# Exclusive sums of the fourth unit by one logarithm, and engine orders written out as tables, in a gated recurrence with a squared-ReLU layer behind it

## The chip, the cores and the metric

The kernel runs on one core of one Trainium2 chip. The metric is the device time of one execution in microseconds (us), lower is better. The engines are PE (matrix products), DVE (vector), ACT (activation functions, also copies), POOL (general purpose) and SP, which here only issues DMA transfers. POOL issues some transfers as well. Each engine runs its own list of instructions strictly in order and waits on semaphores for the others.

## The reference

A recurrence with a decay for each channel runs over 768 tokens, for 4 batches, 8 heads and a head size of 48. Its output, as 3072 tokens of 384 values, goes through two dense layers with a squared ReLU between them.

```python
for t in range(S):
    state = alpha[:, :, t, :, None] * state + np.einsum('bhd,bhe->bhde', k[:, :, t], v[:, :, t])
    y[:, :, t] = np.einsum('bhd,bhde->bhe', q[:, :, t], state)
...
h = x @ w_in            # 384 -> 2048
g = np.maximum(h, 0.0) ** 2
return (g @ w_out).astype(np.float32)      # 2048 -> 384
```

Inputs and output are float32; inside, products are taken in bf16.

## The kernel before

**Tiling.** The work is cut into 12 *units* of 256 tokens: unit g is batch g % 4, time chunk g // 4. A partition holds two neighbouring tokens, j = 0 and 1, for all heads. Units 0 to 3 are the first chunk of each batch, so the "fourth unit" is unit 3. Every step of a unit is an operation with a short name; the number behind it is the unit, and further numbers are parts of it.

**Front of a unit** (`front`, `decays_by_pair`, lines 670 to 765). `lda ldk ldq ldv` load alpha, k, q, v into one of four `raw` buffers (L568; on SP, for unit 2 on POOL). The decay from the start of a chunk to each token is the exponential of a running sum of log alpha. From unit 2 on: `pr` multiplies alpha of both tokens of a pair (L675 on DVE, L677 on POOL); `ln` takes the logarithm (L678); `m1i` multiplies by a triangular matrix of ones on PE (L684), which gives the inclusive sums in a PSUM bank `psW`; `ei`, `ea` and `ec` are exponentials of them (L695, L697, L700); `bk` multiplies by alpha of j = 1 (L704). The queries of j = 0 need the *exclusive* sums, and there are two ways to them, chosen by `if g < RATIO` at L706 with `RATIO = 4` (L424):

- units 2 and 3: a second triangular product `m1s` with the strict triangle (L684 again, `lstr`), `es` as its exponential (L709), and `aq`, a multiplication by alpha of j = 0 (L713);
- units 4 to 11: `lm`, the logarithm of alpha of j = 1 (L717), `lb`, the inclusive sums less that (L719, on DVE), and `es` as the exponential (L721).

Unit 0 is done by halves of the heads (`front_by_heads`, L584 to L641), unit 1 by token (L646 to L667). `vc` casts v to bf16 (L613, L741 on POOL, L742 on ACT). `ekm` and `eqm` multiply keys and queries by their exponentials (L620, L746, L751, on DVE). `tr` transposes them: on PE with an eviction `et` for units 0 to 2 (L632 with L639 and L641, L774 with L781 and L783), by DMA on SP for the others (L762).

**Attention and state.** `p` are the scores (L940), `mk` masks them (L951, on DVE), `kv` are the products for the state (L811), `sa`, `sc` and `sd` bring the state up to date (L904 to L917). `y` is the output of the recurrence (L832 and L843, in units 0 to 2 L872 and L879). From y2 on, one y holds the kv of the next unit too, so y2 waits for vc3. `xe` evicts the output (L971), `xt` transposes it (L986 on PE, L992 by DMA), `xv` evicts that for units 0 to 3 (L998, L1000).

**Dense layers.** For each unit eight parts `s1` (L1042, six matmuls each) go into two PSUM banks in turn, `re` is the ReLU (L1050 on ACT, L1052 on DVE), `sq` squares two parts at once, or one for the last two (1024 or 512 elements, L1060 on DVE, L1063 on POOL, L1064 on ACT). `s2` is the second layer (L1089, four matmuls each, first index the half of the tokens), `oe` evicts (L1097, L1099), `out` stores. The second half of the tokens of the last unit is cut in two (L1012 to L1021). The weights come by POOL in two parts each (`win`, `wout`, L539); the first four `s1` of a unit read only the first part of `win`.

**What sets the order.** `add` records operations with their reads and writes, engines that could run them (`alts`) and a priority. `schedule` (L159) runs a list scheduler over estimated costs, by priority plus a shift for each name from a table `SHIFT` (L49), and so picks engine and order. `fill` (L271) puts matmuls of zeros into early gaps of PE (L1143). `place` (L298) derives the semaphore waits; the order is fixed when the program is built. Loads also have gates of their own (`AFTER`, L1119, and `BEHIND`, L551): `win` waits until alpha of unit 1 has landed, POOL's loads of unit 2 until v of unit 1 has, the loads of unit 3 until the first `wout` has, and from unit 5 on a load waits for a step of the unit before (alpha for its `ln`, k for its `ekm`, q and v for its `tr0`).

Of the kernel before, what the change touches and what calls it, by code (L numbers as in the profile page):

```python
# [2 lines left out]

# [3 lines left out]
ALU = mybir.AluOpType  # L7
# [7 lines left out]
class Op:  # L15


    __slots__ = ("alts", "eng", "fn", "cost", "prio", "deps", "idx", "lag", "sem", "start", "end", "pos", "name",
                 "users", "ndeps", "mode", "ready", "land")

    def __init__(self, alts, prio, name):
        self.alts, self.prio, self.name = alts, prio, name
        self.eng = self.fn = self.cost = None
        self.deps = {}
        self.lag = 0
        self.sem = None
        self.users = []
        self.pos = None
        self.mode = ("F", "F")
        self.ready = 0.0  # L30
        self.start = self.end = self.land = None


class Program:

    HOP = 35
    PE_LATENCY = 170
    DMA_FIRST = {"sp": 1300, "act": 1300, "pool": 2000}  # L40
    PACKET = (("win", 172), ("wout", 490), ("ld", 22), ("tr", 18), ("xt", 18), ("out", 125))
    SBUF_ONLY = ("pr", "bk", "aq", "ekm", "eqm", "sq", "sb", "sd")
    BIAS = {"pool": 300}
    DMA_LAST = {"sp": 800, "act": 800, "pool": 1900}
    SWITCH = 95
    HALVED = {"qks": 3, "kqt": 3, "raw": 3, "ek": 3, "eq": 3, "acm": 2, "laf": 2}
    AFFINITY = 2500

    SHIFT = {  # L49
# [55 lines left out]
    }  # L105

# [1068 lines left out]
```

## Time and profile before

| | |
|---|---|
| median of 3 runs | 175.18 us (174.51 to 175.5) |
| span of the profiled execution | 174.47 us (the page rounds to 174.5) |
| around the span, median less span | 0.71 us |
| granted TensorE clock | 1.000 |
| first matmul of the dense layers (L1042) | starts at 18.46 us |
| last matmuls (L1012), by the chain of waits | 169.49 to 172.14 us |

The profiled execution's own time isn't given apart from its span; the median stands for it. A row of the page's groups reads: line, engine, operation, output<-inputs, shape, count, busy us, mean ns of one, idle time before them and who ended it. In the timeline, a row is: start us, length us, engine, line, operation, in brackets how long the engine was idle before and who released it. The chain of waits is the chain of work that ended last, followed back from the end; its rows are: start us, us, what. PE overlaps matmuls, so what one costs is read from start to start and not from its length.

### The profile page before, as it was taken

How to read it: one execution, taken by the hardware profiler on the slowest of the kernel's cores; microseconds unless marked ns; L12 is line 12 of the kernel's file. 1: busy time of each engine (PE TensorE's matmuls, PEld its weight loads, DVE VectorE, ACT ScalarE, POOL GpSimd, SP SyncE). 2: the span in 40 equal slices, each digit the busy share in tenths (PEclk: the TensorE clock that was granted, in tenths of full speed). 3: DMA queues.
4: the chain of work that ended last, by engine and by line, in shares of the span. 5: the costliest groups of instructions: out<-in, count | busy, mean ns of one | idle time of the engine just before them, and what ended most of it. 6: DMA issues, size and time to landing. Idle time of an engine off the chain costs nothing.

```text
span 174.5 us, 5094 instructions
## 1 busy us (share of the span) xinstructions
PE 169.1 (97%) x2237; PEld 130.5 (75%) x2237; DVE 121.3 (70%) x197; ACT 117.6 (67%) x211; POOL 18.8 (11%) x28
## 2 busy tenths in 40 slices
PE   7989999999999999999999999999999999999994
PEld 2556898856886697777788886778788697688773
DVE  5497799797967869866778966868849726322230
ACT  3848698868869569768768757378668564566440
POOL 3159010022102120000100000000200000000000
DMA  5999999979998999798998897999899690040022
GB/s 139 324 297 190 274 303 216 230 208 280 274 229 125 274 235 188 200 222 151 278 212 211 228 196 180 275 201 251 201 214 208 115 196 4 0 135 4 10 80 90
DMA packets 74743, 33.36 MB, mean 191 GB/s; under 512 B 71649, under 2 KB 71905, under 8 KB 74721
## 3 DMA queue, kind: packets, MB, share of 16 engines
q1 hardware_dynamic: 73184, 28.32, 71.4%
q0 software_dynamic: 1536, 4.72, 12.1%
q8 instruction: 17, 0.28, 0.7%
q14 instruction: 6, 0.04, 0.1%
HBM read 25.17 MB, written 4.72 MB: 171 GB/s over the span
## 4 chain that ended last, share of the span: by engine, by line
PE 56%; DMA 26%; ACT 6%; DVE 4%; SPq 3%; POOL 2%; issue 1%
PE psO L1089 22%; PE psWH L1042 22%; DMA raw<-in_v_dram 9%; DMA wout<-in_moe_w_out_dram 8%; DMA raw<-in_alpha_dram 5%; DMA raw<-in_q_dram 5%; SPq L568 3%; PE psO L1143 2%; POOL raw L568 2%; ACT rr L1050 2%; PE psX L843 2%; PE psX L1012 2%; ACT vbf L742 1%; PE psZ L811 1%; PE psX L832 1%; PE psX L940 1%
## 5 line engine op out<-in xcount | busy, mean ns | idle before, releaser
L1042 PE MATMUL psWH<-xt,win 128*128 128x256 bf16 x576 | 73.9, 275 | 0.5 <-ACT rr L1050 0.2
L1042 PEld LDWEIGHTS psWH<-xt,win 128*128 128x128 bf16 x576 | 65.0, 145 | 6.2 <-DVE rr L1052 1.6
L1089 PE MATMUL psO<-wout,gt 128*128 128x384 bf16 x368 | 68.9, 326 | 0.0
L1050 ACT ACTIVATE rr<-psWH 128x512 bf16<-128x512 f32 x83 | 48.9, 596 | 21.5 <-PE psWH L1042 20.0
L1089 PEld LDWEIGHTS psO<-wout,gt 128*128 128x128 bf16 x368 | 34.8, 98 | 18.3 <-DVE gt L1060 0.2
L1060 DVE TENSOR_TENSOR gt<-rr 128x1024 bf16<-128x1024 bf16 (+1 forms) x47 | 28.4, 608 | 25.1 <-ACT rr L1050 24.5
L951 DVE TENSOR_TENSOR pm<-psX,caus 128x1024 bf16<-128x1024 f32 x12 | 14.6, 1220 | 2.4 <-PE psZ L940 2.1
L951 DVE TENSOR_TENSOR pm<-psZ,caus 128x1024 bf16<-128x1024 f32 x12 | 14.6, 1216 | 1.5 <-PE psZ L940 1.4
L1097 ACT ACTIVATE osb<-psO 128x384 f32<-128x384 f32 x19 | 9.3, 489 | 6.8 <-PE psO L1089 6.3
L971 ACT ACTIVATE xbf<-psX 128x768 bf16<-128x768 f32 x12 | 9.7, 806 | 5.0 <-PE psX L832 4.1
L746 DVE TENSOR_TENSOR qks<-raw,eq 128x384 bf16<-128x384 f32 x18 | 10.3, 605 | 3.0 <-DMA raw<-in_q_dram 3.0
L1143 PE MATMUL psO<-zero 128*128 128x512 bf16 (+1 forms) x37 | 10.5, 417 | 1.3 <-DVE zero L489 1.3
L741 POOL CAST vbf<-raw 128x768 bf16<-128x768 f32 x4 | 3.7, 930 | 71.5 <-DMA raw<-in_v_dram 71.5
L1064 ACT ACTIVATE gt<-rr 128x512 bf16<-128x512 bf16 (+1 forms) x13 | 10.8, 828 | 0.4
L751 DVE TENSOR_TENSOR qks<-raw,ek 128x768 bf16<-128x768 f32 x11 | 10.7, 969 | 0.4 <-ACT ek L663 0.3
L1052 DVE TENSOR_SCALAR rr<-psWH 128x512 bf16<-128x512 f32 x13 | 8.9, 687 | 2.0 <-PE psWH L1042 1.6
L742 ACT ACTIVATE vbf<-raw 128x768 bf16<-128x768 f32 x7 | 5.9, 845 | 3.5 <-DMA raw<-in_v_dram 3.5
L717 ACT ACTIVATE la<-raw 128x384 f32<-128x384 f32 x8 | 4.2, 523 | 5.3 <-DMA raw<-in_alpha_dram 5.2
L1143 PEld LDWEIGHTS psO<-zero 128*128 128x128 bf16 x37 | 3.5, 108 | 4.6 <-issue 1.9
L906 DVE TENSOR_TENSOR smd<-psZ,sbd 128x384 bf16<-128x384 f32 x8 | 4.4, 554 | 3.4 <-PE psX L832 3.4
L675 DVE TENSOR_TENSOR prd<-raw 128x384 f32<-128x384 f32 x7 | 4.0, 569 | 2.9 <-DMA raw<-in_alpha_dram 2.9
L678 ACT ACTIVATE lab<-prd 128x384 bf16<-128x384 f32 x10 | 5.2, 520 | 1.1 <-POOL prd L677 0.6
(115 smaller groups left out, 165.9 us busy)
## 6 DMA issues: line engine op xcount, KB each, us to landing
raw<-in_alpha_dram SPq DMA_DIRECT2D x11, 384.0 KB, 4.2
raw<-in_k_dram SPq DMA_DIRECT2D x11, 384.0 KB, 5.1
raw<-in_q_dram SPq DMA_DIRECT2D x11, 384.0 KB, 4.2
raw<-in_v_dram SPq DMA_DIRECT2D x11, 384.0 KB, 4.8
out_dram<-osb SPq DMA_DIRECT2D x11, 384.0 KB, 4.3
win<-in_moe_w_in_dram POOLq DMA_DIRECT2D x2, 768.0 KB, 9.9
wout<-in_moe_w_out_dram POOLq DMA_DIRECT2D x2, 768.0 KB, 15.2
raw<-in_alpha_dram POOLq DMA_DIRECT2D x1, 384.0 KB, 9.7
```

The costliest lines, as they stand in the source:

```text
L746: add("dve", lambda e, j=j, dst=dst: e.tensor_tensor(dst, RAW[r][:, 2, :, j, :].rearrange("p (n x) d -> p n x d", x=2), EQ[la][:, j].rearr ...
L751: add("dve", lambda e, a=a, E=E: e.tensor_tensor(QKS[qs][:, a, :, :, 0:D], RAW[r][:, 1 + a].rearrange("p h j d -> p j h d"), E[la][:].rear ...
L951: add("dve", lambda e, hf=hf, psT=psT: e.tensor_tensor(PM[pm][:, hf].rearrange("p r n j t -> p (r n) (j t)"), psT[:, :, :].rearrange("p r ...
L971: add("act", lambda e: e.activation(XBF[x2][:], psX[:, :, 0:HD], AF.Copy), act_ns(2 * HD), p0 + 6100, reads=[("ps", "X", 0), ("ps", "X", 1 ...
L1042: ins = pe.matmul(psH[hb][:, i * T:(i + 1) * T], WIN[:, kk, hidden(fj)], mov, start=(kk == 0), stop=(kk == KT - 1))
L1050: add("act", lambda e, hb=hb, rr=rr: e.activation(rr, psH[hb], AF.Relu), act_ns(512), pu + 600, reads=[("ps", "H", hb)], writes=[("rr", rb ...
L1052: alts={"dve": (lambda e, hb=hb, rr=rr: e.tensor_scalar(rr, psH[hb], 0.0, None, ALU.max), dve_ns(512))})
L1060: add("dve", lambda e, dst=dst, sq=sq: e.tensor_tensor(dst, sq, sq, ALU.mult), 148 + k * 267, pu + 1200, reads=[("rr", rb, h) for h in ran ...
L1064: "act": (lambda e, dst=dst, sq=sq: e.activation(dst, sq, AF.Square), act_ns(k * 512))})
L1089: ins = pe.matmul(psS, GT[gt][:, fj, j, :], WOUT[:, fj, :], start=(fj * parts % FT == 0), stop=((fj + 1) * parts % FT == 0))
L1097: add("act", lambda e, j=j, psS=psS: e.activation(OSB[ob][:, j], psS, AF.Copy), act_ns(DM), ps_ + 700, reads=[keyS], writes=[("osb", ob, j ...
L1143: pr.fill(lambda n: lambda pe: pe.matmul(psO[:, 0:n], ZERO[:, 0:128], ZERO[:, 0:n], skip_group_check=True), ((512, 216, 420), (256, 109, 2 ...
```

## The change

`RATIO` goes from 4 to 3, so unit 3 takes the way of units 4 to 11: `m1s3` and `aq3` fall away, `lm3` and `lb3` are new. `schedule`, `fill` and `SHIFT` are taken out. A table of names for each engine, `TABLES`, now says what runs where and in what order; `+512` and `+256` are the matmuls of zeros. `arrange` takes engine and place from it, and `sequence` finds an order of all for `place`. The reads of one PSUM bank, which `add` orders among each other, no longer make an instruction wait for another of its own engine (`shared`). All operations now have names; nothing else of what they compute is changed.

```diff
-    RATIO = 4
+    RATIO = 3
...
             if k[0] == "ps":
                 for r in self.readers.get(k, ()):
-                    op.deps.setdefault(r, False)
+                    if r not in op.deps:
+                        op.deps[r] = False
+                        op.shared.add(r)
...
-                if d.sem is None and d.eng == o.eng == "pe":
+                if d.sem is None and d.eng == o.eng and (o.eng == "pe" or not raw and d in o.shared):
                     continue
...
+    def arrange(self, tables, make, after):
+
+        named = {o.name: o for o in self.ops}
+        assert len(named) == len(self.ops)
+        self.order = {}
+        for e, text in tables.items():
+            self.order[e] = []
+            for x in text.split():
+                if x[0] == "+":
+                    o = Op({e: (make(int(x[1:])), 0)}, 0, "fill")
+                    o.idx = len(self.ops)
+                    o.deps = {after: True}
+                    self.ops.append(o)
                 else:
...
+                    o = named.pop(x)
+                o.eng = e
+                o.fn, o.cost = o.alts[e]
+                o.pos = len(self.order[e])
+                self.order[e].append(o)
+        assert not named, sorted(named)
...
+TABLES = {
+    "act": """
+        ln1_0 ln0_0 table ei0_0 ea0_0 ei1_0 xcaus ea1_0 ec0_0 vc0 ec1_0 ln1 et01_0 et11_0 ei1 ea1 xe0 ec1 et0_1
+        re0_0 re0_1 ln2 sq0_1 xe1 ei2 ea2 ec2 re0_6 re0_7 es2 re1_0 re1_1 re1_2 re1_3 et0_2 et1_2 sq1_5 sq0_7
+        re1_7 ln3 oe0_0 ei3 lm3 ea3 re1_6 ec3 vc3 es3 oe0_1 lm4 xe2 ln4 ei4 ea4 ec4 sa3 re2_0 es4 re2_1 oe1_0
...
+    "dve": """
+        zero zcaus1 zlstr zlinc zqk0 zla0 zcaus zones zown zqk2 zident zqk1 ekm0_0 eqm0_0 zla1 zown0 ekm1_0
+        et00_0 zown1 et10_0 eqm1_0 zlb0 sa0 mk0_0 mk1_0 ekm1 sc0 zlb1 eqm1 xv0 et1_1 mk1_1 mk0_1 sa1 re0_2 re0_3
+        re0_4 re0_5 xv1 bk2 sq0_6 sc1 ekm2 aq2 eqm2 re1_4 re1_5 sq1_3 mk1_2 mk0_2 sq1_7 sa2 sc2 ekm3 lb3 eqm1_3
...
+    "pe": """
+        +512 +512 +512 +512 +512 +512 +512 +512 m11_0 m10_0 +512 +512 +512 +512 +512 +256 tr00_0 tr10_0 +512
+        +512 +512 +256 +256 kv0 tr01_0 tr11_0 p0_0 m11 p1_0 +512 +512 +512 +512 +512 +256 +256 y0 tr0_1 +512 xt0
+        tr1_1 +512 +512 +512 +256 p0_1 s1_0_0 s1_0_1 kv1 s1_0_2 s1_0_3 y1 m1i2 s1_0_4 s1_0_5 xt1 s1_0_6 s1_0_7
+        m1s2 s1_1_0 s1_1_1 s1_1_2 s1_1_3 tr0_2 s1_1_4 s2_0_0_0 s1_1_5 tr1_2 s2_0_0_1 s1_1_6 p0_2 s1_1_7 s2_0_0_2
+        s2_0_0_3 m1i3 kv2 s2_0_1_0 s2_0_1_1 s2_0_1_2 s2_0_1_3 y2 s2_1_0_0 s2_1_0_1 xt2 m1i4 s2_1_0_2 s1_2_0
...
+        s1_8_4 s1_8_5 s2_7_1_2 s2_7_1_3 s1_8_7 p0_10 s1_8_6 s2_8_0_0 s1_9_1 s2_8_0_1 s1_9_0 s2_8_0_2 s2_8_0_3
+        s1_9_3 s1_9_2 y10 s2_8_1_0 s2_8_1_1 s1_9_4 s1_9_5 s2_8_1_2 s2_8_1_3 s1_9_7 s1_9_6 p0_11 s2_9_0_0 s1_10_0
+        s1_10_1 s2_9_0_1 s2_9_0_2 s2_9_0_3 s1_10_3 s1_10_2 s2_9_1_0 y11 s1_10_4 s2_9_1_1 s2_9_1_2 s2_9_1_3
+        s1_10_5 s1_10_6 s2_10_0_0 s1_10_7 s2_10_0_1 s1_11_0 s2_10_0_2 s2_10_0_3 s1_11_2 s1_11_1 s2_10_1_0
...
+    "pool": """
+        slstr scaus1 slinc scaus sident win0 lda2 win1 ldk2 sd0 wout0 vc1 ldq2 ldv2 pr2 sq0_3 wout1 sq0_5 vc2
+        sq1_1 pr3 sd1 bk3 bk4 sd3 vc4 bk5 sq2_3 sq2_6 pr6 sd4 vc6 pr7 sd5 bk7 bk8 sq5_7 bk9 sq6_3 vc9 pr10 sq7_1
+        vc10 sq8_1 bk11 sq9_7 sq9_5 sq10_5 sq11_6
+    """,
+    "sp": """
+        lda0 ldq0 ldk0 ldv0 lda1 ldv1 ldk1 ldq1 lda3 ldq3 ldk3 ldv3 lda4 ldv4 ldq4 ldk4 tr1_3 lda5 tr0_3 ldk5
+        tr0_4 out0_1 tr1_4 ldq5 ldv5 out1_1 lda6 tr0_5 tr1_5 ldk6 ldq6 xt4 ldv6 lda7 ldk7 tr1_6 tr0_6 out2_1 xt5
...
```

The same places of the order before, as the scheduler gave it. ACT starts with the table load, the copy of the mask (`xcaus`) and the two logarithms of unit 0. DVE runs sa0 and sc0 between the two masks of unit 0. POOL runs vc0, win0, win1, sd0, the four loads of unit 2, wout0, wout1, sd1 and then mostly pr and vc; it has no squares. SP loads alpha, k, q, v in that order in each of the first units. PE has nine matmuls of zeros ahead of the first m1 products, m1i2 comes behind s1_0_7, m1 of unit 1 behind p1_0. ACT has 83 ReLUs and 13 squares (after: 67 and 25), DVE 13 and 47 (after: 29 and 22), POOL no squares (after: 13) and no bk (after: 7).

More of the change, by code (lines that the diff above doesn't have):

```diff
@@ L1 @@
-import heapq
-import itertools
 import concourse.bass as bass
@@ L15 @@
 class Op:
-    __slots__ = ("alts", "eng", "fn", "cost", "prio", "deps", "idx", "lag", "sem", "start", "end", "pos", "name",
-                 "users", "ndeps", "mode", "ready", "land")
+    __slots__ = ("alts", "eng", "fn", "cost", "prio", "deps", "idx", "lag", "sem", "pos", "name", "mode", "shared")
     def __init__(self, alts, prio, name):
@@ L26, in __init__ @@
         self.sem = None
-        self.users = []
         self.pos = None
         self.mode = ("F", "F")
-        self.ready = 0.0
-        self.start = self.end = self.land = None
+        self.shared = set()
 class Program:
[L38 to L45, printed above, removed]
-    HALVED = {"qks": 3, "kqt": 3, "raw": 3, "ek": 3, "eq": 3, "acm": 2, "laf": 2}
-    AFFINITY = 2500
-    SHIFT = {
[55 rows of a table removed]
-    }
+    HALVED = {"qks": 3, "kqt": 3, "raw": 3, "ek": 3, "eq": 3, "acm": 2, "laf": 2}
     def __init__(self, nc):
@@ L271, in fill @@
-    def fill(self, make, sizes, until, after, cold):
-        new = []
-        t = after.land + self.HOP
-        cold += t
-        for o in self.order["pe"]:
-            while t < until:
-                slow = 2 if t < cold else 1
-                fits = [(n, c) for n, c, gap in sizes if o.start - t > gap + (slow - 1) * c]
-                if not fits:
-                    break
-                n, c = fits[0]
-                f = Op({"pe": (make(n), c)}, 0, "fill")
-                f.idx = len(self.ops)
-                f.eng, f.fn, f.cost = "pe", make(n), c
-                f.start, f.end = t, t + c * slow
-                f.deps = {after: True}
-                self.ops.append(f)
-                new.append(f)
-                t = f.end
-            new.append(o)
-            t = max(t, o.end)
-        for i, o in enumerate(new):
-            o.pos = i
-        self.order["pe"] = new
+    def arrange(self, tables, make, after):
[10 more added lines that the diff above has]
+                    self.ops.append(o)
+                else:
+                    o = named.pop(x)
[4 more added lines that the diff above has]
+        assert not named, sorted(named)
@@ new lines, in sequence @@
+    def sequence(self):
+        done, seq = set(), []
+        at = {e: 0 for e in self.order}
+        while len(seq) < len(self.ops):
+            before = len(seq)
+            for e, ops in self.order.items():
+                while at[e] < len(ops) and all(d in done for d in ops[at[e]].deps):
+                    o = ops[at[e]]
+                    done.add(o)
+                    seq.append(o)
+                    at[e] += 1
+            assert len(seq) > before, {e: ops[at[e]].name for e, ops in self.order.items() if at[e] < len(ops)}
+        return seq
@@ L301, in place @@
         waits = {}
-        seq = sorted(self.ops, key=lambda o: (o.start, o.idx))
+        seq = self.sequence()
+        rank = {o: i for i, o in enumerate(seq)}
         needed = set()
@@ L322, in place @@
             mine = []
-            for d in sorted(want.values(), key=lambda d: -d.start):
+            for d in sorted(want.values(), key=lambda d: -rank[d]):
                 s, p = stream(d), place_of(d)
@@ L351, in emit @@
         stores = {}
-        for o in sorted((o for o in self.ops if o.name.startswith("out")), key=lambda o: o.start):
-            stores.pop(o.sem[0], None)
-            stores[o.sem[0]] = o
+        for o in self.order["sp"]:
+            if o.name.startswith("out"):
+                stores[o.sem[0]] = o
         final = [(self.dma_sems[k], self.value[o]) for k, o in stores.items()]
@@ L496, in bass_gla_recurrent__then__act_relu_squared_kernel @@
         add("dve", fill(LAF[i][:, :, :, D:64].rearrange("p j h d -> p (j h) d"), 0.0), 250, -1e6 - 10,
-            writes=[("laf", i)])
-        add("dve", fill(LAB[i][:, :, D:64], 0.0), 150, -1e6 + 20, writes=[("lab", i)])
+            writes=[("laf", i)], name=f"zla{i}")
+        add("dve", fill(LAB[i][:, :, D:64], 0.0), 150, -1e6 + 20, writes=[("lab", i)], name=f"zlb{i}")
     for i in range(NQKS):
         add("dve", fill(QKS[i][:, :, :, :, D:64].rearrange("p a j h d -> p (a j h) d"), 0.0), 500, -1e6 + 10,
-            writes=[("qks", i, 0), ("qks", i, 1)])
+            writes=[("qks", i, 0), ("qks", i, 1)], name=f"zqk{i}")
     flat = [t[:].rearrange("p a b c -> p (a b c)") for t in (CAUS, CAUS1)]
@@ L504, in bass_gla_recurrent__then__act_relu_squared_kernel @@
                           (flat[0], "caus", 1.0), (flat[1], "caus1", 1.0), (ONES2[:], "ones", 1.0)):
-        add("dve", fill(buf, val), 100, -2.5e6, writes=[(key,)])
-    add("pool", select(LINC[:], ALU.is_ge, 0.0, 0, [[1, 128]], -1), 300, -1e6, reads=[("linc",)], writes=[("linc",)])
-    add("pool", select(LSTR[:], ALU.is_gt, 0.0, 0, [[1, 128]], -1), 300, -1e6, reads=[("lstr",)], writes=[("lstr",)])
-    add("dve", fill(OWN[:], 0.0), 100, -2e6, writes=[("own",)])
-    for part in (OWN[0:64, 0:H:2], OWN[64:128, 1:H:2]):
-        add("dve", fill(part, 1.0), 100, -2e6, reads=[("own",)], writes=[("own",)])
-    zero = add("dve", fill(ZERO[:], 0.0), 300, -3e6, writes=[("zero",)])
+        add("dve", fill(buf, val), 100, -2.5e6, writes=[(key,)], name="z" + key)
+    add("pool", select(LINC[:], ALU.is_ge, 0.0, 0, [[1, 128]], -1), 300, -1e6, reads=[("linc",)], writes=[("linc",)], name="slinc")
+    add("pool", select(LSTR[:], ALU.is_gt, 0.0, 0, [[1, 128]], -1), 300, -1e6, reads=[("lstr",)], writes=[("lstr",)], name="slstr")
+    add("dve", fill(OWN[:], 0.0), 100, -2e6, writes=[("own",)], name="zown")
+    for x, part in enumerate((OWN[0:64, 0:H:2], OWN[64:128, 1:H:2])):
+        add("dve", fill(part, 1.0), 100, -2e6, reads=[("own",)], writes=[("own",)], name=f"zown{x}")
+    zero = add("dve", fill(ZERO[:], 0.0), 300, -3e6, writes=[("zero",)], name="zero")
     add("pool", select(IDENT[:], ALU.not_equal, 1.0, 0, [[-1, 128]], 1), 300, -1e6 + 5, reads=[("ident",)],
-        writes=[("ident",)])
+        writes=[("ident",)], name="sident")
     for c, key in enumerate(("caus", "caus1")):
         add("pool", select(flat[c], ALU.is_ge, 0.0, 128 * c, [[-1, 2], [1, 2], [2, 64]], -2), 400, -1e6 + 7,
-            reads=[(key,)], writes=[(key,)])
+            reads=[(key,)], writes=[(key,)], name="s" + key)
     add("act", lambda e: e.activation(flat[1][0:64], flat[0][0:64], AF.Copy), 400, -1e6 + 8,
-        reads=[("caus",), ("caus1",)], writes=[("caus1",)])
+        reads=[("caus",), ("caus1",)], writes=[("caus1",)], name="xcaus")
     def bcast(t, row, dims):
@@ L1141, in bass_gla_recurrent__then__act_relu_squared_kernel @@
             moe(g)
-    pr.schedule()
-    pr.fill(lambda n: lambda pe: pe.matmul(psO[:, 0:n], ZERO[:, 0:128], ZERO[:, 0:n], skip_group_check=True),
-            ((512, 216, 420), (256, 109, 250)), min(o.start for o in pr.order["pe"] if o.name.startswith("s1_")), zero, 4600)
+    pr.arrange(TABLES, lambda n: lambda pe: pe.matmul(psO[:, 0:n], ZERO[:, 0:128], ZERO[:, 0:n], skip_group_check=True),
+               zero)
     pr.place()
```

144 lines of the change are left out of this document (38 added, 106 removed), and 55 rows, old and new, of the table SHIFT.

## The prediction

> **What bounds the kernel now.** I read the page first. Three of its lines, and one of its DMA issues:
>
> ```profile
> PE 169.1 (97%) x2237; PEld 130.5 (75%) x2237; DVE 121.3 (70%) x197; ACT 117.6 (67%) x211; POOL 18.8 (11%) x28
> ...
> L1042 PE MATMUL psWH<-xt,win 128*128 128x256 bf16 x576 | 73.9, 275 | 0.5 <-ACT rr L1050 0.2
> L1089 PE MATMUL psO<-wout,gt 128*128 128x384 bf16 x368 | 68.9, 326 | 0.0
> ...
> raw<-in_alpha_dram POOLq DMA_DIRECT2D x1, 384.0 KB, 9.7
> ```
>
> The two matmul groups of the dense layers hardly wait, and no other engine passes 70%. Busy time overlaps, so next I took the timeline of PE, start to start: six L1042 matmuls without a wait take 0.656 us, four of L1089 0.65 us. From the first L1042 at 18.46 us on, PE loses against these only 2.8 us: 1.3 before the output of unit 2 at 40.42 and 1.5 after it. So a new order can save at most these 2.8 us and whatever it takes from the first 18.46 us. In the timeline, engine by engine, the start and one loss read:
>
> ```profile
> 0.80 1.28 ACT L483 ACT_TABLE_LOAD   x1 [0.80 <-PEq L1160]
> 4.33 0.94 ACT L584 ACTIVATE laf<-raw 128x384 bf16<-128x384 f32 x2 [0.93 <-DMA raw<-in_alpha_dram]
> 6.04 0.49 ACT L605 ACTIVATE ek<-psX 128x384 f32<-128x384 f32 x1 [0.78 <-PE psX L596]
> ...
> 7.08 0.56 DVE L620 TENSOR_TENSOR qks<-raw,eq 128x384 bf16<-128x384 f32 x1
> 7.95 1.21 DVE L620 TENSOR_TENSOR qks<-raw,ek 128x384 bf16<-128x384 f32 x1
> ...
> 7.93 0.82 POOL L613 CAST vbf<-raw 128x768 bf16<-128x768 f32 x1 [4.98 <-DMA raw<-in_v_dram]
> ...
> 114.34 0.53 ACT L717 ACTIVATE la<-raw 128x384 f32<-128x384 f32 x1 [2.42 <-DMA raw<-in_alpha_dram]
> ...
> 115.41 0.88 PE L1042 MATMUL psWH<-xt,win 128*128 128x256 bf16 x6 [0.19 <-ACT rr L1050]
> ```
>
> The reader is to see three things. The table is loaded while ACT has nothing to do. The same DVE multiply takes 0.56 us alone and 1.21 beside POOL's cast. And at 114 us a relu stands behind a logarithm that waits for alpha, so PE waits for the relu. The chain of waits shows where the first 40 us go:
>
> ```profile
> 8.04 1.14 DVE qks L620
> ...
> 13.21 3.52 POOL raw L568 x4
> 16.73 13.68 DMA wout<-in_moe_w_out_dram
> ...
> 34.10 5.31 DMA raw<-in_v_dram
> 39.44 0.85 ACT vbf L742
> 40.29 0.14 issue
> 40.42 0.36 PE psX L872 x8
> ```
>
> SP issues the loads of unit 3 only when the first half of w_out has landed (30.41). v of unit 3 lands at 39.41, its cast ends at 40.29, and y2 (which also holds unit 3's state matmuls) waits for it.
>
> **The change, part by part.**
>
> *Exclusive sums of unit 3.* One triangular product goes from PE: 162 ns start to start (L684), and DVE's multiply by alpha (0.56). ACT gains a logarithm (0.52), DVE a subtraction (0.55). PE keeps 0.16; the rest lies on engines with 30% to spare.
>
> *Start of ACT.* The explicit table load now stands behind the two first logarithms, and the build puts another load ahead of them. The first costs nothing: ACT is idle until alpha lands at 4.24. The second runs from 5.27 to 6.55, and the first exponential goes from 6.04 to 6.55: +0.51. Behind the load queue all exponentials of unit 0, the copy of the mask (0.42, now behind the third exponential) and v's cast (0.85, from POOL). What follows a load when the next instruction is ready, no row shows: behind the load at 0.80 ACT rests 0.90 us, for POOL's mask. So the extra is 0 to 0.90; I take 0, as that wait has a named cause. The Trainium skill speaks against this edit: its page "ScalarE: Activation LUTs", section "What ACT_TABLE_LOAD costs", gives about 1283 ns for the load plus a drain of about 1380 ns for every switch of set. The trace agrees on the first (1.28); by the second, the sum below would lose 1.38 us of its gain.
>
> *What the start gains.* POOL's cast no longer stretches the DVE multiply (1.21 to 0.56, -0.65). Added up from these rows: the logarithm of unit 1 ends at 10.85 (now 10.98), its m1 product stands ahead of p1_0 and ends near 12.05 (now 12.75); the second mask product ends at 13.9 (now 13.40), because ACT's evictions of unit 0 (0.60 each) now follow that logarithm. On DVE sc0 (0.56) moved behind the key product of unit 1, so the query product ends at 16.35 (now 15.5). The last eviction is DVE's (0.68) and no longer ACT's (1.02). Scores of unit 1: 17.7 (now 17.88). First L1042: 18.28 (now 18.46). w_in's first half lands at 9.37 + 8.5 = 17.9 and just covers this.
>
> *Weights and loads.* POOL's queue becomes w_in, a2, w_in, k2, sd0, w_out, v cast, q2, v2, pr2, w_out. Its a2 waits for v1, which SP now issues second of unit 1's four (k1's place, issue 5.45, landing near 10.3 with the 4.8 of the page); sd0 waits for sc0 until 15.35, and behind it queue w_out, the cast, q2, v2 and pr2. The first transfers outlast that: these four land until 24.7 now (k2: issue 14.11 + 10.6). w_out passes q2 and v2, which take from 24.7 to 26.85 (15.86 + 11.0): it lands near 28.3 and not 30.4, and unit 3's loads leave 2.1 us earlier. The second half of w_in, behind a2, lands near 22.85 (a2 now: 13.16 + 9.7); s1_0_4 would come at 22.7, so it costs 0.15.
>
> *Up to y2.* Unit 2's front: pr2 on POOL ends at 20.6, m1 of unit 2 goes ahead of s1_0_4, and re1_0 comes behind three exponentials, so s1_1_2 waits about 0.5. y2 then stands at 39.5 on PE, but v3's cast follows the exponentials of unit 3 on ACT and ends at 39.9, though v3 lands near 37.4. y2 starts at 40.0 (now 40.42): **-0.42**, with the 0.16 and 0.18 from above in it.
>
> *After y2.* The 1.5 us lost there are: 0.27 before y5 at 74.21 and 0.16 before y7 at 99.52 (v's cast), 0.41 and 0.27 at 115.4 and 117.2 (relu and square behind late fronts), 0.16 at 65.88, 0.22 inside the last output. The tables take 16 relus from ACT (83 to 67), put 13 squares on POOL and with them the v cast that y5 waits for (unit 6; that of unit 8 stays on ACT), and the loads have 2.1 us more in hand. I count 0.27, 0.41 and 0.27 (0.95) as gone and the other 0.54 as kept: a choice, with 1.5 gained as one end and new waits, which no row excludes, as the other (rival 3).
>
> *POOL's squares and products.* 13 squares, seven bk, two pr and two sd products are new there. No square on POOL is in the trace; nearest rows: a two-input product of 128x384 takes 0.82 alone and 1.04 on average, a cast of 768 0.82 to 0.93. For 1024 elements that gives 1.1 (the cast, by elements) to 2.8 (1.04 by elements); I take 2.2 (0.82 by elements, the uncovered product being nearest). Cover: most readers come over 3 us behind the relu. The tightest are sq9_5 behind sq9_7 (0.77 + 1.1 + 2.2 = 4.1 against 4.0 us of PE work in between) and sq10_5 (3.1 against 3.3).
>
> *Waits between readers of one PSUM bank* on one engine are dropped: the engine runs in order anyway, I cost it at nothing.
>
> The end is unchanged: 2.3 us from the last matmul (172.14) to the end of the span.
>
> **The sum.** The profiled execution spans 174.47; the median of the runs is 175.18, so 0.71 lies around it. 174.47 - 0.42 - 0.95 = 173.10, and with 0.71: **173.8 us**, 0.8% less. All losses gone would be 174.47 - 0.18 - 0.16 - 2.76 = 171.4, so 172.1.
>
> **Rivals.** What a measurement of this kernel can tell from no change is about 0.5%, that is 174.30 to 176.06.
>
> 1. *Gain given back.* The start is ahead by 0.42, but PE loses as much later as now: 174.8. For it: the loads of unit 5 onwards are chained to the unit before (a behind its logarithm, q and v behind its transposes), so a head start may not last. Against: fewer relus stand behind ACT's loads of alpha. Chance 0.16.
> 2. *The table load stalls ACT further.* The extra 0.90 of the bound above reaches the first L1042 at 19.2, and everything behind it: 174.7, not told from no change. Against: no row shows a pause that has no other cause. By the page named above it would be 173.8 + 1.38 = 175.2. Chance 0.07.
> 3. *Slower: POOL and DVE in each other's way.* Eleven products of 1.0, nine squares of 2.2 and four of 1.1 are 35 us more on POOL. DVE's products from SBUF are about 35% of a unit (ekm 0.97, two eqm 0.6, squares, pr, sd, some 4.4 of 12.5 us), so some 12 us of them fall beside POOL, and the 1.21 for 0.56 says they stretch by that overlap. One such stretch of now (the square at 22.56, 1.36 for 0.69) was followed by 0.49 lost on PE at 25.9 to 28.4. If PE pays a fifth of 12 us, 2.4, and the later 0.95 isn't gained: 174.47 - 0.42 + 2.4 + 0.71 = 177.2. It decides from 1.3 us paid on (0.42 + 0.88). For it: DVE and ACT wait for one another's halves of a square. Against: DVE loses 19 of its long squares and seven bk. Chance 0.25.
> 4. That the change doesn't do what it says: the sums of unit 3 do pass to the logarithm and the orders are as written, so no chance of its own.
>
> **Numbers.** The forecast has 0.52. Faster 0.52; within 0.5% 0.23 (rivals 1 and 2); slower 0.25. Range 172.1 to 177.2: from no losses left to the price of rival 3, beyond which I leave its upper part and little below. The forecast's own range is 172.1 to 174.3.
>
> **What would show it.** Two table loads, the second ending at 6.55 with an exponential right behind it (if later: rival 2). The first L1042 within 0.3 of 18.28. The DVE multiplies of unit 0 at 0.56. w_out's first half landing near 28.3. y2 near 40.0. On PE, no losses before the output of unit 5 nor near 115. POOL's squares near 2.2 us of 1024; if DVE's products from SBUF average well over 0.7 and waits for squares appear on PE, rival 3. I would be wrong if PE lost over 1 us between 18 and 40, or if one late load moved a whole unit.

## The result, and the profile after

The changed kernel takes **176.38 us** (median of 15 runs, 175.37 to 177.86), the kernel before on the same chip 174.99 (15 runs, 174.51 to 177.31). The ratio is **1.007, 95% interval 1.0045 to 1.0095**: 0.7% slower, where 0.8% faster was forecast. Medians count every run; the ratios leave out the occasional execution that is over 1.5% longer than the fastest of its kernel.

The profiled execution of after took 176.47 us with a span of 174.4. The lines of its page that answer to those shown of before:

```profile
PE 167.9 (96%) x2230; PEld 130.0 (75%) x2230; DVE 119.1 (68%) x185; ACT 110.5 (63%) x200; POOL 52.5 (30%) x53
...
L931 PE MATMUL psWH<-xt,win 128*128 128x256 bf16 x576 | 75.2, 275 | 1.5 <-DMA xt<-xbf 0.7
...
L978 PE MATMUL psO<-wout,gt 128*128 128x384 bf16 x368 | 69.4, 326 | 0.0
...
L952 POOL TENSOR_TENSOR gt<-rr 128x1024 bf16<-128x1024 bf16 (+1 forms) x13 | 21.9, 1687 | 40.0 <-DVE rr L941 20.4
```

ACT and DVE gave work to POOL (POOL 18.8 to 52.5 us), as the diff says. The dense matmuls (L931, formerly L1042) still wait little (1.5 us in sum, 0.5 before), but what they wait for most has changed: no longer a relu, but `xt` by DMA. The timeline of after at the start, ACT first:

```profile
4.14 0.94 ACT L473 ACTIVATE laf<-raw 128x384 bf16<-128x384 f32 x2 [0.61 <-DMA raw<-in_alpha_dram]
5.09 1.28 ACT L372 ACT_TABLE_LOAD   x1
6.38 0.49 ACT L494 ACTIVATE ek<-psX 128x384 f32<-128x384 f32 x1
...
8.24 0.84 ACT L503 ACTIVATE vbf<-raw 128x768 bf16<-128x768 f32 x1
```

The exponential stands right behind the second table load: 5.09 + 1.28 = 6.37, and it starts at 6.38. The DVE multiplies of unit 0 and the first dense matmuls:

```profile
7.38 0.55 DVE L509 TENSOR_TENSOR qks<-raw,eq 128x384 bf16<-128x384 f32 x1
8.00 0.55 DVE L509 TENSOR_TENSOR qks<-raw,ek 128x384 bf16<-128x384 f32 x1
...
18.15 1.53 PE L931 MATMUL psWH<-xt,win 128*128 128x256 bf16 x12 [0.53 <-DMA win<-in_moe_w_in_dram]
22.94 1.29 PE L931 MATMUL psWH<-xt,win 128*128 128x256 bf16 x10 [0.20 <-DMA win<-in_moe_w_in_dram]
```

The multiply of the keys takes 0.55 and no longer 1.21. The first dense matmul could go 0.53 earlier than it does, but the first half of `w_in` is not there; nor is the second half, later on. The output of unit 2 starts at 39.67. From there on, this is where the chain of waits leaves PE:

```profile
116.15 0.61 ACT rr L939
116.76 0.49 SPq L881
...
117.30 0.58 SPq L457
...
117.92 0.58 SPq L998
...
118.55 6.14 DMA raw<-in_v_dram
...
124.74 0.83 POOL vbf L630
...
125.71 0.27 PE psX L721 x8
...
126.86 0.96 DVE xbf L862
127.84 5.12 DMA xt<-xbf
...
133.00 0.88 PE psWH L931 x6
```

The reader is to see that the chain runs through SP's own queue: the alpha of unit 11 and an output stand ahead of v of unit 10 (118.55), whose landing releases the cast and the output of unit 9 (125.71, PE idle for 0.70). The first row, a relu, is only what the view infers: the transfer `xt8` (L881) was being issued from 115.23 on, and ACT had ended the eviction that it reads at 113.87. The output of unit 9 is evicted and transposed by a DMA, and PE stands again before the first dense part of unit 9 (133.00, 0.74). SP's timeline of after shows why this queue is late; start, length and line of each issue:

```profile
105.34 2.88 SPq L651 DMA_TRANSPOSE kqt<-qks  x1
108.27 0.58 SPq L457 DMA_DIRECT2D raw<-in_k_dram  x1
112.53 0.37 SPq L457 DMA_DIRECT2D raw<-in_q_dram  x1
112.94 0.58 SPq L998 DMA_DIRECT2D out_dram<-osb  x1
113.56 1.63 SPq L651 DMA_TRANSPOSE kqt<-qks  x1
115.23 2.02 SPq L881 DMA_TRANSPOSE xt<-xbf  x1
117.30 0.58 SPq L457 DMA_DIRECT2D raw<-in_alpha_dram  x1
117.92 0.58 SPq L998 DMA_DIRECT2D out_dram<-osb  x1
118.55 1.71 SPq L457 DMA_DIRECT2D raw<-in_v_dram  x1
```

Between 108.85 (k of unit 10 issued) and 112.53 SP issues nothing. q of unit 10 waits, by the gate in `BEHIND`, until the first transpose of unit 9 has landed (112.51), and two outputs, the second transpose, `xt8` and two loads (alpha of unit 11, v of unit 10) stand behind it. In the waits of SP's queue (what, us in total, times, longest) this is

```profile
SPq L457 <- DMA kqt<-qks: 4.8, 3, 3.7
```

4.8 us in three waits, the longest 3.7. In a further profile of the kernel before (run `e0_before`, below) the same row reads

```profile
SPq L568 <- DMA kqt<-qks: 0.7, 1, 0.7
```

because there both transposes, an output and `xt` stand ahead of q, as SP's timeline of `e0_before` shows:

```profile
108.79 5.52 SPq L762 DMA_TRANSPOSE kqt<-qks  x2
114.35 1.31 SPq L1109 DMA_DIRECT2D out_dram<-osb  x1
115.70 1.26 SPq L992 DMA_TRANSPOSE xt<-xbf  x1
117.01 0.57 SPq L568 DMA_DIRECT2D raw<-in_q_dram  x1
117.63 0.64 SPq L568 DMA_DIRECT2D raw<-in_v_dram  x1
121.90 0.37 SPq L568 DMA_DIRECT2D raw<-in_alpha_dram  x1
```

SP of the kernel before stands still for as long, only elsewhere:

```profile
SPq L568 <- DMA raw<-in_q_dram: 14.8, 7, 3.6
```

The longest of these waits is the one from 118.27 to 121.90. Behind it stand alpha and k of unit 11, and PE loses nothing behind it in this execution. So the length of a wait doesn't tell what it costs.

### The profile page after: what moved, and what is told of

Same layout as the page of the kernel before. It is cut to its first block, busy times and chain, and to the rows that moved or that the text cites. A ratio compares the mean times of both kernels' runs of the same rounds, so it can differ in the third digit from the quotient of the medians.

```text
span 174.4 us, 5091 instructions
## 1 busy us (share of the span) xinstructions
PE 167.9 (96%) x2230; PEld 130.0 (75%) x2230; DVE 119.1 (68%) x185; ACT 110.5 (63%) x200; POOL 52.5 (30%) x53
## 4 chain that ended last, share of the span: by engine, by line
PE 76%; DMA 16%; SPq 3%; POOL 2%; issue 1%; DVE 1%; ACT 0%
PE psWH L931 32%; PE psO L978 31%; DMA win<-in_moe_w_in_dram 7%; DMA raw<-in_v_dram 4%; DMA xt<-xbf 3%; DMA raw<-in_alpha_dram 3%; SPq L457 2%; PE psX L732 2%; PE psZ L700 2%; PE psX L721 2%; PE psX L829 2%; PE psX L901 2%; PE psZ L829 1%; PE psWH L573 1%; PE psZ L663 1%
## 5 line engine op out<-in xcount | busy, mean ns | idle before, releaser
L931 PE MATMUL psWH<-xt,win 128*128 128x256 bf16 x576 | 75.2, 275 | 1.5 <-DMA xt<-xbf 0.7
L931 PEld LDWEIGHTS psWH<-xt,win 128*128 128x128 bf16 x576 | 65.6, 145 | 7.9 <-DMA xt<-xbf 1.5
L939 ACT ACTIVATE rr<-psWH 128x512 bf16<-128x512 f32 x67 | 39.4, 596 | 34.7 <-PE psWH L931 34.3
L952 POOL TENSOR_TENSOR gt<-rr 128x1024 bf16<-128x1024 bf16 (+1 forms) x13 | 21.9, 1687 | 40.0 <-DVE rr L941 20.4
L941 DVE TENSOR_SCALAR rr<-psWH 128x512 bf16<-128x512 f32 x29 | 19.8, 690 | 18.6 <-PE psWH L931 18.3
L953 ACT ACTIVATE gt<-rr 128x1024 bf16<-128x1024 bf16 (+1 forms) x25 | 22.4, 903 | 1.6 <-DVE rr L941 1.3
L949 DVE TENSOR_TENSOR gt<-rr 128x512 bf16<-128x512 bf16 (+1 forms) x22 | 14.5, 663 | 8.1 <-ACT rr L939 8.1
L591 POOL TENSOR_TENSOR ek<-ek,raw 128x384 f32<-128x384 f32 x7 | 7.4, 1052 | 25.8 <-ACT ek L584 25.8
L566 POOL TENSOR_TENSOR prd<-raw 128x384 f32<-128x384 f32 x5 | 5.0, 1008 | 12.4 <-DMA raw<-in_alpha_dram 12.4
L988 DVE COPY osb<-psO 128x384 f32<-128x384 f32 x7 | 3.9, 555 | 4.1 <-PE psO L978 4.1
L584 ACT ACTIVATE ek<-psWH 128x384 f32<-128x384 f32 x10 | 4.9, 491 | 2.6 <-PE psWH L576 1.5
L804 POOL TENSOR_TENSOR sbd<-tmp,acm 128x384 bf16<-128x384 f32 x5 | 5.3, 1051 | 4.2 <-DVE tmp L802 4.2
```

The costliest lines, as they stand in the source:

```text
L931: ins = pe.matmul(psH[hb][:, i * T:(i + 1) * T], WIN[:, kk, hidden(fj)], mov, start=(kk == 0), stop=(kk == KT - 1))
L939: add("act", lambda e, hb=hb, rr=rr: e.activation(rr, psH[hb], AF.Relu), act_ns(512), pu + 600, reads=[("ps", "H", hb)], writes=[("rr", rb ...
L941: alts={"dve": (lambda e, hb=hb, rr=rr: e.tensor_scalar(rr, psH[hb], 0.0, None, ALU.max), dve_ns(512))})
L949: add("dve", lambda e, dst=dst, sq=sq: e.tensor_tensor(dst, sq, sq, ALU.mult), 148 + k * 267, pu + 1200, reads=[("rr", rb, h) for h in ran ...
L952: alts={"pool": (lambda e, dst=dst, sq=sq: e.tensor_tensor(dst, sq, sq, ALU.mult), 200 + k * 840), "act": (lambda e, dst=dst, sq=sq: e.act ...
L953: "act": (lambda e, dst=dst, sq=sq: e.activation(dst, sq, AF.Square), act_ns(k * 512))})
```

## The experiments

Each run has its ratio to the kernel before on the same chip, with a 95% interval. "Loss" is what PE loses against the start-to-start times of the prediction. Each is the median of 6 to 12 runs.

**e0_before**: the kernel before, unaltered.

> The kernel before once more, for a second profile and for the span of each execution. Theory A (the profiled execution of before was an unlucky one, whose late loads near 72, 98 and 114 us are not typical): most spans near 173.0, about 2.0 us below the time of their execution, and PE's losses after 40 us under 1 us. Rival B (that execution was typical, and 0.7 us lie around the span): spans near 174.3, the same losses in the same places.

175.00 us, ratio 1.000 (0.997 to 1.003). Its profiled execution took 174.89 us with a span of **173.2**, so 1.69 lies around the span and not 0.71. Its first L1042 starts at 17.44, the output of unit 2 at 40.02. It loses nothing before the outputs of units 5 and 7, and some 0.5 us near 115 (0.25 and 0.27, where the execution shown lost 0.41 and 0.27). The execution that the prediction was worked out from had a span of 174.47: a long one of the kernel before.

**e1_v10**: v of unit 10 right behind q.

```diff
-tr0_9 ldk10 ldq10 out5_1 tr1_9 xt8 lda11 out6_1 ldv10
+tr0_9 ldk10 ldq10 ldv10 out5_1 tr1_9 xt8 lda11 out6_1
```

> The changed kernel with one move on SP: the load of v of unit 10 is issued right behind that of q, ahead of a store, a transpose, an xt transpose and a load. Theory A (the changed order loses its lead because v10 is issued 6 us behind q10 and y9 waits for its cast, and xt9 after it): the wait of 1.1 us before y9 goes and most of the 0.9 us in the dense part behind xt9 too, 1.0 to 1.9 us less than the changed kernel, so 0.996 to 1.001 of before. Rival B (POOL's new squares and products cost it, spread over all units): no change beyond 0.3 us, 1.005 to 1.009 of before.

176.56 us, 1.005 (1.002 to 1.009). The wait for v is gone and another has come: the second transpose is issued at 114.61 instead of 113.56, and the scores of unit 9 wait for it. The longest of PE's waits (what, us in total, times, longest):

```profile
PE psX L829 <- DMA kqt<-qks: 2.6, 1, 2.6
```

That wait is longer than the 1.05 us by which the issue came later; why the transpose also took longer to land is not shown. So v's place alone was not the cause: whatever stands behind q can be late.

**e2_table**: the table loaded first, once (`table ln1_0 ln0_0` for `ln1_0 ln0_0 table`).

> The changed kernel with the explicit table load at the head of ACT again, so that only one load is left. Theory A (the first dense product waits for the first half of w_in anyway, 0.5 us in the trace, so the front of unit 0 has cover): within 0.2 us of the changed kernel, 1.005 to 1.009 of before, and the first dense product still at 18.1. Rival C (the second load costs its 0.5 us to the end): 0.5 us less, 1.003 to 1.005.

176.27 us, 1.005 (1.002 to 1.009). The load goes back to 0.81, and still the first exponential starts at 6.42, now waiting for the sums on PE. The second load costs the end nothing that can be measured.

**e3_squares**: POOL's 13 squares on DVE, the table otherwise the same.

> The changed kernel with all 13 squares of POOL done by DVE, at places of its order near the relus that feed them. Theory A (loads of unit 10): about the same, 1.004 to 1.010 of before, as DVE gains 8 us of work but has 30% free. Rival B (POOL beside DVE): the multiplies on DVE get shorter, and 1 to 2 us go, 0.996 to 1.002 of before.

176.03 us, 1.005 (1.002 to 1.008), with 1.4 lost to a square on DVE behind a late load. The span is as long without POOL's squares (median 174.3, as in after). Since this run has a loss of its own, it doesn't clear them by itself; i5 below does. The time around the span fell, which is taken up below.

**f0_tables**: the order of before written out as tables in the changed program (with its rule for waits), unit 3 by the second triangular product.

> The order of before, engine by engine as its scheduler gave it, written out as tables in the changed program, with RATIO = 4: the new way of placing waits alone. Every theory expects no change: 0.997 to 1.003 of before. If the dropped waits count for anything, below 0.997.

175.52 us, 1.000 (0.996 to 1.004): tables instead of a scheduler, and the waits dropped between readers of one bank, are worth nothing.

**f1_sp, f2_before_sp, f3_sp_win**: the queue of SP swapped between the two orders, from unit 3's transposes on; in f3 also `win1` ahead of alpha of unit 2.

> The changed kernel with SP's order of before from the transposes of unit 3 on: both transposes of a unit together, xt ahead of q and v. Theory D (in the changed order SP sits on q of the next unit, which waits for the first transpose to land, while the second transpose or xt stands behind it, and PE pays 1 to 2.6 us in one place or another in most executions): the waits after 60 us go, 0.996 to 1.001 of before. Rival E (the orders of the computing engines leave less dense work in hand, whatever SP does): 1.004 to 1.009, as the changed kernel.

> The order of before with SP's order of the changed kernel from the transposes of unit 3 on. Theory D: it brings the loss along, 1.004 to 1.012 of before, with waits of 1 us or more on PE for transposes, v or xt after 60 us. Rival E: 0.998 to 1.003.

> As the changed kernel with SP's order of before, and on POOL the second half of w_in ahead of the load of alpha of unit 2. If the wait for that half (0.2 to 1.0 us at the fifth dense part in four traces) is the other loss of the changed order, it goes and 0.2 to 0.9 us with it: 0.991 to 0.998 of before by theory D, 1.000 to 1.006 by rival E. If unit 2's front then comes late instead, as in the kernel with the other SP order.

200.1 us, 1.133 (1.125 to 1.141); 186.8, 1.062 (1.056 to 1.068); 204.4, 1.160 (1.153 to 1.167). All three expectations were far off: an order of SP's queue is only good with the order of the other engines that it was made with. In f1, output 2 waits at 70.4 us for an eviction, and `xt4`, q and v of unit 6 stand behind it; the longest of SP's waits:

```profile
SPq L995 <- ACT osb L983: 26.6, 6, 8.4
```

These runs tell how badly a queue of SP and the orders of the other engines can misfit, but not which wait costs the changed kernel its 0.7%.

**g1_sp9**: both transposes of unit 9 together, and `xt8` ahead of q.

```diff
-tr0_9 ldk10 ldq10 out5_1 tr1_9 xt8 lda11 out6_1 ldv10
+tr0_9 tr1_9 ldk10 xt8 ldq10 ldv10 out5_1 lda11 out6_1
```

> The changed kernel with one stretch of SP's table reordered. There the queue read: first transpose of unit 9, k10, q10, output 5, second transpose, xt8, alpha 11, output 6, v10; q10 waits for the landing of the first transpose, so in the profiled execution SP issued nothing from 108.85 to 112.5 us and all behind it came late. Now: both transposes, k10, xt8, q10, v10, output 5, alpha 11, output 6. Theory D (what is lost is mostly this stretch: 0.76 us before y9 and 0.8 to 0.9 before the first dense part of unit 9): both losses under 0.3, 175.2 us, ratio to before 1.000. Rival (the whole order of the loads has less slack, and one late transfer is met at another place of each execution): this place is clean, another one loses 0.7 to 1.5 us between 45 and 135, ratio 1.004 to 1.009.

178.65 us, 1.014 (1.009 to 1.020): worse. SP's timeline shows the new wait:

```profile
107.84 5.56 SPq L648 DMA_TRANSPOSE kqt<-qks  x2
...
116.29 1.21 SPq L878 DMA_TRANSPOSE xt<-xbf  x1
117.55 0.58 SPq L454 DMA_DIRECT2D raw<-in_q_dram  x1
...
121.29 0.37 SPq L454 DMA_DIRECT2D raw<-in_alpha_dram  x1
```

Now `xt8` waits for its eviction until 116.29, and alpha of unit 11 leaves at 121.29 instead of 117.30; its logarithm holds PE up for 1.0 us at 129. PE also waits 1.1 us at 123.5 for a square on ACT, and 1.0 us for a mask at 63, far ahead of the stretch that was changed. The stretch was given another wait at its head; how much of the 1.4% that is, one profile doesn't tell.

**g2_log**: the order of before as tables, with the logarithm for unit 3 alone.

> The order of before, as tables, with the logarithm way for unit 3 alone: the triangular product and the multiplication go, the logarithm stands behind ei3 on ACT and the subtraction in the multiplication's place on DVE. Theory (the logarithm alone changes 0.16 us of PE and nothing of the end, what is slower is the order): ratio 0.997 to 1.001 to before, 174.6 to 175.3 us. Rival (the longer way through ACT and DVE makes es3 late, and with it the transposes and scores of unit 3): a loss of over 0.4 us near 45 to 55 us, ratio 1.003 to 1.007.

175.82 us, 0.999 (0.995 to 1.003): the part of the change that is in its name moves nothing that can be measured.

**h1_front, h2_rest, i3_cut**: the tables cut in time. Before the cut all engines go by one order, behind it by the other. h1: the new order to the output of unit 2 (39.7 us). h2: the new order from there on. i3: the new order to the output of unit 7 (97.5 us).

> The tables cut at the output of unit 2 on PE (39.7 us): all five engines go by the changed kernel's order before it, and by the order of before behind it (one square stays on DVE at the seam). Theory D (the later part of the new order is what costs, the front gives 0 to 0.5 us): ratio 0.997 to 1.000, 174.5 to 175.1 us, no loss over 0.6 between 45 and 135. Rival E (the new front is what costs: the second half of w_in behind the alpha of unit 2, and loads that leave 3 us earlier): ratio 1.004 to 1.009, with the wait of 0.2 to 1.0 us at 23 us in it.

> The reverse: the order of before on all engines up to the output of unit 2 (40 us; unit 3 by the second triangular product), the changed kernel's order behind it. Theory D: the loss stays, ratio 1.005 to 1.011, 176.0 to 177.0 us, with 0.8 to 2.6 us lost at one or two places between 45 and 135 behind a late load or transpose. Rival E: ratio 0.998 to 1.002. A third case, that the new rest needs the 3 us that unit 3's loads leave earlier: more than 1.011, with the losses at the first transposes (45 to 60).

> The tables cut later, at the output of unit 7 (97.5 us): the changed kernel's order on all engines before it, the order of before behind it. Cut at 39.7 us the ratio was 0.998, uncut it is 1.007. If the last third is what costs (as in the profiled execution of the changed kernel, where the losses were at 125.7 and 133): 0.997 to 1.001, and its losses behind 98 us sum to under 0.6. If the middle costs: 1.004 to 1.009, with the losses between 45 and 98. If the cost is spread, halfway, 1.001 to 1.004.

h1: 0.998 (0.995 to 1.002). h2: 179.1 us, 1.017 (1.012 to 1.023). i3: 174.55 us, **0.997 (0.994 to 0.999)**. So, in the median, the new order costs nothing up to 97.5 us and may gain a little; all of the loss comes behind. In h2 the rest finds its loads later than it was made for: unit 3's second transpose is issued at 46.91 and not at 43.97, and PE waits 2.91 us for it at 53.27. That the rest needs the earlier start of the new front is read from this one profile.

**i1_gate, i2_before_gate, i5_gate10, i4_cut_gate, i6_after**: the gate. In i1, from unit 5 on, q and v wait for the key product of the unit before and no longer for its first transpose; all tables are as they were. i2 is the same in the order of before (f0). i5 changes this for q of unit 10 alone, i4 puts i1's gate into i3, i6 is the changed kernel again.

```diff
-    BEHIND = {"a": "ln", "k": "ekm", "q": "tr0_", "v": "tr0_"}
+    BEHIND = {"a": "ln", "k": "ekm", "q": "ekm", "v": "ekm"}
```

> The changed kernel; from unit 5 on the loads of q and v wait for the key product (ekm) of the unit before, as k's do, and no longer for its first transpose. Nothing else is moved, and the loads still go into one of four buffers that is long free. In the changed kernel SP stood 4.8 us for landings of transposes (once 3.7, ahead of the second transpose of unit 9), in the kernel before 0.7. Theory D (this wait, with the second transpose, xt and v behind it, makes the late transfers): it goes, no loss over 0.4 us near 125 and 133, ratio 0.998 to 1.002. Rival F (the order itself has too little slack, the wait only shows it): q and v leave earlier and meet the transposes, ratio 1.004 to 1.015, with 0.7 to 2 us lost at one place between 45 and 135.

> The control: the order of before as tables (unit 3 by the second triangular product), with the same earlier gate for q and v. There SP stood only 0.7 us for landings of transposes, since both transposes, an output and xt stand ahead of q. Both theories: ratio 0.997 to 1.004. If it is 0.995 or less, the gate costs the kernel before too, and i1_gate's gain says nothing of the new order.

> The changed kernel with one wait changed: only the load of q of unit 10 waits for the key product of unit 9 and no longer for its first transpose. Theory D, narrow (this one wait carries the loss): as with all gates lifted, ratio 0.997 to 1.002. Rival G (it is spread over units 5 to 11): most of the loss stays, 1.003 to 1.008.

> The changed kernel's order to the output of unit 7 (97.5 us) and before's behind it, with the earlier gate for q and v of all units. If cut and gate take away the same loss (theory D): no faster than the cut alone, ratio 0.995 to 0.999, 174.2 to 175.0 us. If the gates of units 5 to 9 cost something of their own (rival G): 0.990 to 0.994.

> The changed kernel again, unaltered, beside the two others on one chip. By its first result 1.007; all theories: 1.003 to 1.010, with losses of 0.7 to 2 us at one or two places behind late transfers between 45 and 135 us, not all at the places of its first profile.

| run | us | ratio to before | interval |
|---|---|---|---|
| i1_gate | 175.34 | 1.000 | 0.996 to 1.003 |
| i2_before_gate | 175.07 | 1.000 | 0.997 to 1.002 |
| i5_gate10 | 175.28 | **0.9995** | 0.9963 to 1.0028 |
| i4_cut_gate | 174.92 | 0.999 | 0.996 to 1.002 |
| i6_after | 176.60 | **1.0069** | 1.0042 to 1.0096 |

i5 and i6 ran on one chip and differ in one wait of one load. Their intervals do not meet: **this wait carries the loss**, 1.32 us of the 1.47 between i6 and the kernel before (175.13 there). SP's timeline of i5, to be held against that of after:

```profile
107.75 0.58 SPq L454 DMA_DIRECT2D raw<-in_k_dram  x1
108.37 1.16 SPq L454 DMA_DIRECT2D raw<-in_q_dram  x1
109.57 2.16 SPq L995 DMA_DIRECT2D out_dram<-osb  x1
111.78 1.63 SPq L648 DMA_TRANSPOSE kqt<-qks  x1
113.95 1.21 SPq L878 DMA_TRANSPOSE xt<-xbf  x1
115.21 0.58 SPq L454 DMA_DIRECT2D raw<-in_alpha_dram  x1
116.07 0.36 SPq L995 DMA_DIRECT2D out_dram<-osb  x1
116.47 0.43 SPq L454 DMA_DIRECT2D raw<-in_v_dram  x1
```

q leaves at 108.37 and no longer at 112.53, right behind k; v of unit 10 at 116.47 and no longer at 118.55. Of PE's waits in i5, only one is for a transfer:

```profile
PE psWH L928 <- DMA win<-in_moe_w_in_dram: 0.6, 1, 0.6
```

and in i6, where q waits again, the wait for v's cast is back at the same place (125.7 us):

```profile
PE psX L718 <- POOL vbf L627: 0.4, 1, 0.4
```

i2 says that the earlier gate by itself gives the kernel before nothing. i4 says that cut and gate take away the same loss, and do not add up. i3 is the only version whose interval lies below 1; that it beats the kernel before is likely rather than settled, since its interval ends at 0.999 and i4, which differs by the gate, reaches 1.002.

Single executions of the new order lose at other places too. The profile of e2 has 1.0 us before the output of unit 4 (62.98), behind DVE's masks, which come late after q of unit 5; that of i4, with the gate lifted, has 0.65 at this output (62.34) and 0.82 for `xt` at 70.64. What is shown of q of unit 10 is shown of the median.

**Around the span.** The time of a run less its span was 1.68 to 1.81 us in every run of before and of the kernels f0, f2, g2, h1, i2, i3, i4 and e3. In those with the new order of POOL to the end (after, e1, e2, f1, f3, g1, h2, i1, i5, i6) it was 1.7 in some runs and 1.9 to 2.2 in most: in the mean 1.97 in i5 and 2.10 in i6, against 1.74 of before beside them. e3 differs from after by its 13 squares on POOL only, and has 1.74; i3 keeps those squares that come before 97.5 us, and has 1.75. So POOL's squares add 0.2 to 0.4 us outside the span in the mean, and it seems to be those behind 97.5 us (i3 differs there in more than the squares). Which one does it, and how, was not tried.

## Why the prediction was wrong

**The base of the sum failed first.** "The profiled execution spans 174.47; the median of the runs is 175.18, so 0.71 lies around it." In every run here 1.7 to 2.2 us lie around the span. The execution shown had therefore taken about 174.47 + 1.7 = 176.2, a long one, and the spans of before have a median of 173.2 to 173.6 in four of the five sets of runs (174.3 in one). I took losses of a long execution off the time of a median one. In the profiles of e0, f0, g2 and i2, which have its order at the start, the first L1042 stands at 17.4 to 18.2 and not at 18.46. And e0 has only part of the 0.95: some 0.5 near 115 and none before y5. With 173.3 as a base, y2 at 40.0 as e0 has it anyway, and 0.5 for 0.95, my own steps would have given 173.3 - 0.5 + 1.7 = 174.5, or 0.3% less: inside the 0.5% that the prediction counts as no change.

**Up to y2 the steps held, and are worth little.** Table load, multiplies, the first half of `w_out` (unit 3's loads leave at 27.50, from 28.3 forecast and 30.65 in e0), and y2 at 39.67 (40.0 forecast, 40.42 in the execution shown, 40.02 in e0, 39.77 in i2). Two sizes were off. The first half of `w_in`, which "just covers" the first dense part, held it up by 0.53 in after, but not in i3, i5 and i6. The second half, costed at 0.15, cost 0.2 in after and 0.6 to 0.9 in i3, i5 and i6. That alpha of unit 2, ahead of it on POOL, is the cause is not shown: in the profile of f3 that half goes first and PE no longer waits for it, but waits 0.84 for the first half instead. h1 shows what is left of the gain: a ratio of 0.998, not told from 1.

**The forecast's second term failed on a wait that I did not cost.** "I count 0.27, 0.41 and 0.27 (0.95) as gone", since "the loads have 2.1 us more in hand". The relus and the old casts did stop being late. But the new table of SP puts q of unit 10 ahead of the second transpose of unit 9, and q has a gate on the landing of the first. The prediction followed POOL's queue at the start entry by entry, and did not do this for SP's behind unit 4, though it names the gate in its first rival, and the new table was in view. The wait costs 3.7 us of SP; PE lost 0.70 and 0.74 behind it in the profile of after. Lifting that gate alone brought the median span from 174.5 (i6) to 173.25 (i5), 1.25 us, with 173.3 for before: the whole of what the span had lost. One sign that the prediction set itself, "if one late load moved a whole unit", came true in v of unit 10.

**Rivals.** *Gain given back* (174.8) came nearest. It names the gate ("q and v behind its transposes"), but only as a reason why a head start may not last. That other transfers stand behind the load that waits, it does not have, nor the size: the head start was used up, and 1.2 us more. *The table load stalls ACT further*: no. The exponential follows 0.01 us behind the load, and e2 without the second load is no faster than 1.005. The Trainium skill, page "ScalarE: Activation LUTs", section "What ACT_TABLE_LOAD costs", adds about 1380 ns of drain for every switch to a different set; this trace shows none behind this load, and it does not tell whether the two loads took different sets. *POOL and DVE in each other's way* (177.2) got the sign and not the cause; that the measured time lies inside the range is owed to the price of this rival, and so to luck. POOL's squares of 1024 take 1.97 us in the mean, and the lengths are as that rival priced them. But PE waits for no square in the profile of after, e3 without them is at 1.005, and i5 with all of them at 0.9995, so they cost the span nothing that can be measured. What they do cost, 0.2 to 0.4 us around the span, no part of the prediction had.

**Open**: why squares on POOL lengthen the time outside the span; and how much of i3's 0.3% would stand with more runs.

## What to carry to other kernels

When an order changes, go through the queue that issues the transfers as through any engine: for each entry ask what it waits for, and what stands behind it. A load that waits may cost nothing by coming late itself (PE took up the scores of unit 10 only at 130.16), and still be dear by what stands behind it in the queue and is needed sooner. With nothing urgent behind it, a wait as long (3.6 us) cost the kernel before nothing.

Before working out a sum, ask whether the profiled execution is a typical one. If its span lies much closer to the median time than the spans of further executions do to theirs (0.71 against 1.7 us here), it was a long one, and part of its losses is not there to be gained.

Two orders can be compared by cutting them at one time on all engines; swapping one queue alone (1.06 to 1.16 here) tells more of the misfit than of the queue.

## What the runs showed of the hardware

- A load of the activation table between a logarithm and an exponential cost its 1.28 us and no pause behind it (5.09 + 1.28, next start 6.38).
- On SP, a wait at the head of the queue held all behind it. One of 3.7 us, for a transpose that landed 4.3 us after its issue had ended, stood ahead of a load that took 6.1 us to land; lifting it took 1.25 us (0.7%) off the median span. One of 3.6 us in the kernel before, with nothing urgent behind it, cost PE nothing.
- The time around the span is not one number of a kernel: 1.7 to 1.8 us where POOL's last work ends over 40 us before the span does, and in most runs 1.9 to 2.2 where POOL still squares in its last 10 us.
- The same kernel's losses move from run to run: the spans of before went from 172.3 to over 175, and its two profiles start the first dense matmul at 17.44 and 18.46.
